# One word of padding behind each row of the output weights in SBUF

## The chip, the cores and the metric

The kernel runs on one core of one Trainium2 chip. The metric is the time of one execution on the device in microseconds; several executions are taken and their median is given. A measurement of this kernel tells apart differences of about 0.2%. One further execution was profiled; the rows below are from it.

## The reference

Three stages follow each other on 12,160 tokens (2 sequences of 6,080) of 256 features, in float32: a gated scan along each sequence, then two two-layer networks with 2,048 hidden features.

```python
sig = 1.0 / (1.0 + np.exp(-f_logit))
f = lower_bound[None, None, :] + (1.0 - lower_bound[None, None, :]) * sig
i = 1.0 - f
for t in range(S):
    h = f[:, t] * h + i[:, t] * x[:, t]
    y[:, t] = h
...
h = np.maximum(x @ w_in, 0.0)          # first network
x = h * h @ w_out
...
h = x @ w_in                           # second network
g = np.where(h > 0.0, h, np.exp(np.minimum(h, 0.0)) - 1.0)
return g @ w_out
```

## The kernel before, in words

The tokens are cut into units: the first two of 896 and 1,024 tokens (halves of 512 and 384, and of 512 and 512), the others of 1,024 tokens, taken as two halves of 512. In the second network the first unit is halved as 448 and 448. The first network of unit u and the second network of unit u - 3 alternate. Each network's hidden features are worked on in 8 groups g of 256.

TensorE does two kinds of product. Input products (`three`, line 702) multiply a tile of input weights, the ring `ws` (two buffers; in the first units a tile `s` as well), by the activations `xa` and `xb`. Output products (`add_out`, line 938) multiply the output weights `wo` by the hidden activations `g` and add into the PSUM tiles a00 to a11. All numbers are split into a high and a low part in the type float32r, so one product is three matmuls: high by high, high by low, low by high. Every matmul is one weight load of 128 x 128 (stationary operand) and one stream of 512 columns (448 or 384 in a few units) of the moving operand.

The output weights stay in SBUF for the whole kernel: two tiles, `wo0` and `wo1` (line 190), one for each network, of shape 128 x 16 x 2 x 256: for each of 16 blocks j of 128 hidden features the high part's row of 256 words and the low part's row. They are filled once, by ScalarE (high parts, line 404) and VectorE (low parts, line 410), out of the tile `a` of prepared weights. A matmul's stationary operand is half a row:

```python
wh, wl = (wo[m][:, j, x, q * P : (q + 1) * P] for x in range(2))
for p, (y, v) in enumerate(((wh, gh), (wh, gl), (wl, gh))):
    nc.tensor.matmul(a, lhsT=y, rhs=v, ...)
```

A load of 128 words is 512 bytes in each partition. Where tiles lie in SBUF follows from the order of their creation: some small constants, the tile `gap` of `GAP` words (line 187), which nothing reads or writes, then the ring `ws`, then `wo0` and `wo1`, then all other tiles. With `GAP` = 56 the ring begins at byte 2,048 of each partition, `wo0` at 16,384 and `wo1` at 49,152; a row is 1,024 bytes long. All tiles that a matmul of line 702 or 938 reads begin at a multiple of 512 bytes.

The order of the work is written by a planner (`Order`), which lists every step with an engine, a cost in us and a due time, and then gives out the steps engine by engine. Tile addresses do not enter it. For a group g its output products are 12 matmuls in a row (for each of two halves and two 128-column parts: three matmuls; in the first units for each of two parts, two blocks), and the input products stand in groups of 9 and 12.

Of the kernel before, what the change touches and what calls it, by code (L numbers as in the profile page):

```python
# [9 lines left out]
F32R = mybir.dt.float32r  # L10
# [6 lines left out]
P = 128  # L17
# [1 line left out]
CN = 256  # L19
SIZES = ((512, 384), (512, 512))  # L20
LEAD = 2
GAP = 56
BEHIND = 3
AGE = 8.0
ROW = 1 / 2258
# [127 lines left out]
def kernel(  # L153
# [12 lines left out]
    B, S, D = x.shape  # L166
# [3 lines left out]
    KF = DFF // P  # L170
# [15 lines left out]
    one = const.tile([P, P], F32, name="one")  # L186
    const.tile([P, GAP], F32, name="gap")
    pools = {"ws": ctx.enter_context(tc.tile_pool(name="ws_pool", bufs=BUFS["ws"]))}
    outer = ctx.enter_context(tc.tile_pool(name="outer", bufs=1))
    wo = [outer.tile([P, KF, 2, D], F32R, name=f"wo{m}") for m in range(2)]  # L190
    pools |= {
        tag: ctx.enter_context(tc.tile_pool(name=f"{tag}_pool", bufs=n))
        for tag, n in BUFS.items()
# [24 lines left out]
    def new(tag, shape, dtype=F32):  # L218
        return pools[tag].tile(shape, dtype, tag=tag, name=tag)
# [41 lines left out]
    for s in slots:  # L261
        m, u, h, g = s
# [20 lines left out]
    def act(n, psum=False):  # L283
        return (0.05 if psum else 0.09) + n / 1172

    def dve(n, fast=False, psum=False):
        return (0.12 if psum else 0.067) + n / (1920 if fast else 960)

    def chain(due, steps):

        left = sum(st[1] + order.SLACK for st in steps)
        for e, us, what, *rest in steps:
            order.add(e, us, due - left, what, *rest)
            left -= us + order.SLACK
# [3 lines left out]
    def key_of(tag):  # L298
        count[tag] = count.get(tag, -1) + 1
        return tag, count[tag]  # L300
# [5 lines left out]
    def load_w(queue, st, m, kind, c):  # L306
        w = ((w_in1, w_out1), (w_in2, w_out2))[m][kind].bitcast(I32)
        if kind == 1:
            v = w[c * CF : (c + 1) * CF, :].rearrange("(k p) u -> p k u", p=P)
            queue.dma_start(st.rearrange("p k e w -> p k (e w)"), v)  # L310
        elif m == 1:
            v = w[:, 2 * c * CF : 2 * (c + 1) * CF].rearrange("(k p) u -> p k u", p=P)
            queue.dma_start(st.rearrange("p k e w -> p k (e w)"), v)
        else:
            v = w[:, 2 * c * CF : 2 * (c + 1) * CF].rearrange("(p k) u -> p k u", k=KD)
            queue.dma_start(st.rearrange("p k e w -> p k (e w)"), v)

    def weight_sums(q, a):
        nc.vector.tensor_tensor(q[:, 0], a[:, 0], a[:, 2], op=ALU.add)
        nc.vector.tensor_tensor(q[:, 2], a[:, 1], a[:, 0], op=ALU.subtract)  # L320
        nc.vector.tensor_tensor(q[:, 1], q[:, 0], a[:, 1], op=ALU.subtract)
        nc.vector.tensor_tensor(q[:, 3], a[:, 3], q[:, 1], op=ALU.subtract)

    def plain_weights(key):

        if key[0] == "ws":
            return new("ws", [P, 2, NW, P], F32R)[:, :, :4]
        return new("s", [P, 3 * HN], F32R)[:, : 8 * P].rearrange("p (x k i) -> p x k i", x=2, k=4)

    def add_kept_parts(t, x, key, m, c, at, due):  # L330

        w = key_of("wp")

        def high_part(e):
            t["w" + x] = new("wp", [P, 4, P], F32R)
            if e == "ACT":
                nc.scalar.activation(t["w" + x], t[x], AF.Copy)
            else:
                nc.vector.tensor_copy(t["w" + x], t[x])

        def low_part(e):
            nc.vector.tensor_tensor(t[x].bitcast(F32R), t[x], t["w" + x].bitcast(F32), op=ALU.subtract)

        def keep(e):
            nc.sync.dma_start(wd[m][c][:, 0, at : at + 4].bitcast(F32), t["w" + x].bitcast(F32))
            nc.sync.dma_start(wd[m][c][:, 1, at : at + 4].bitcast(F32), t[x])

        chain(due, [
            ["DVE", dve(CE, True), high_part, [key], [w], ("ACT", act(CE))],
            ["DVE", dve(CE), low_part, [w], [key]],  # L350
            ["SP", 1.0, keep, [w, key], [("wd", m, c, at)], None, 512],
        ])

    def add_weights(i, m, kind, c, due, wk=None):
        t = {}

        def load(e):
            t["st"] = new("st", [P, 2, CE // 2, 2], I32)
            if i == 0:
                nc.scalar.activation(warm, warm, AF.Exp)  # L360
            load_w(nc.scalar if i == 0 else nc.sync, t["st"], m, kind, c)
            sv = t["st"].rearrange("p k e w -> p (k e) w")
            t["low"], t["high"] = sv[:, :, 0], sv[:, :, 1]

        def scaled(e):
            t["a"] = new("a", [P, 4, P])
            t["v"] = t["a"].rearrange("p q i -> p (q i)")
            t["vi"] = t["v"].bitcast(I32)
            nc.scalar.activation(t["v"], t["high"].bitcast(F32), AF.Abs, scale=2.0**-112)  # L369

        def low_bits(e):
            nc.scalar.activation(t["low"], t["low"].bitcast(U32), AF.Copy, scale=LOW_SCALE)  # L372

        def magnitude(e):
            nc.vector.scalar_tensor_tensor(t["vi"], t["vi"], 3, t["low"], op0=ALU.logical_shift_left, op1=ALU.bitwise_or)

        def sign(e):
            nc.vector.scalar_tensor_tensor(t["vi"], t["high"], -0x80000000, t["vi"], op0=ALU.bitwise_and, op1=ALU.bitwise_or)

        def sums(e):  # L380
            t["q"] = new("a", [P, 4, P])
            weight_sums(t["q"], t["a"])

        def parts():

            if kind == 0:
                return [(t["a"], ws_t[wk][:, 0], ws_t[wk][:, 1])]
            v = t["a"].rearrange("p (k e) i -> p k (e i)", k=2)
            hi, lo = (wo[m][:, 2 * c : 2 * c + 2, x, :] for x in range(2))
            if m == 0:  # L390
                return [(v, hi, lo)]

            return [
                (v[:, k].rearrange("p (a q j) -> p q a j", a=4, q=KD),
                 *(u[:, k].rearrange("p (q a j) -> p q a j", a=4, q=KD) for u in (hi, lo)))
                for k in range(2)
            ]

        def high_part(e):
            if kind == 0:  # L400
                ws_t[wk] = plain_weights(wk)
            for v, hi, _ in parts():
                if e == "ACT":
                    nc.scalar.activation(hi, v, AF.Copy)
                else:
                    nc.vector.tensor_copy(hi, v)

        def low_part(e):
            for v, hi, lo in parts():
                nc.vector.tensor_tensor(lo, v, hi.bitcast(F32), op=ALU.subtract)  # L410

        def keep(e):
            nc.sync.dma_start(wd[m][c][:, :, 0:4].bitcast(F32), ws_t[wk].bitcast(F32))

        def keep_whole(e):
            nc.sync.dma_start(rd[c], t["a"])

        st, a = ("st", i), key_of("a")
        steps = [
            ["ACT" if i == 0 else "SP", 1.0 if i == 0 else 0.475, load, (), [st], None, 512],  # L420
            ["ACT", act(CE), scaled, [st], [a]],
            ["ACT", act(CE), low_bits, (), [st]],
            ["DVE", dve(CE), magnitude, [st], [a]],
            ["DVE", dve(CE), sign, [st], [a]],
        ]
        if i == 0:
            order.add(*steps[0][:2], -20.0, *steps[0][2:])
            del steps[0]
        if m == 1 and kind == 0:
            q = key_of("a")  # L430
            chain(due - 6.0, [*steps, ["DVE", 4 * dve(P), sums, [a], [q]]])
            add_kept_parts(t, "a", a, m, c, 0, due - 2.0)
            add_kept_parts(t, "q", q, m, c, 4, due)
            return
        w = wk if kind == 0 else ("w", m, c)
        chain(due, [
            *steps,
            ["ACT", act(CE), high_part, [a], [w]],
            ["DVE", dve(CE), low_part, [a], [w]],
        ])  # L440
        if kind == 0:
            order.add("SP", 0.5, due + 16.0, keep, [w], [("wd", m, c, 0)], None, 512)
            order.add("SP", 0.5, due + 10.0, keep_whole, [a], [("rd", c)], None, 256)
# [632 lines left out]
    for kind, s in pe_order:  # L1076
# [3 lines left out]
        m, u, h, g = s  # L1080
# [38 lines left out]
```

## Time and profile before

| | |
|---|---|
| median of 3 executions | 1982.59 us (1982.42 to 1983.38) |
| the profiled execution | 1981.58 us |
| its span, first to last instruction | 1979.8 us |
| TensorE busy | 1962.0 us, 8,716 matmuls and as many weight loads |
| VectorE busy | 1673.0 us |
| ScalarE busy | 1631.8 us |
| HBM traffic | 134 GB/s over the span |

PE is TensorE's matmuls, PEld its weight loads, DVE is VectorE, ACT ScalarE, POOL GpSimd and SP SyncE. L938 is line 938 of the kernel. Matmuls overlap, and their ends are modelled in the profile: their starts are what can be measured. In the timeline a run of like instructions is one row with its start, the time to the end of its last instruction, and its count; the difference of two rows' starts is the time that the first group took on the engine. In the chain of waits a row's second number is the time of the chain that the piece took.

### The profile page before, as it was taken

The numbers are of one execution on the slowest core, as the hardware profiler recorded it, in microseconds if no ns is written. First come the engines' busy times: TensorE is split into PE (matmuls) and PEld (weight loads), VectorE is DVE, ScalarE is ACT, GpSimd is POOL, SyncE is SP. The second block draws the span as 40 slices with busy tenths as digits, with TensorE's granted clock in tenths as the row PEclk, the third lists the DMA queues.
The fourth block names the chain that finished last, engine by engine and source line by source line (L and its number), as shares of the span: only waits on it lengthen the run. The fifth ranks groups of instructions, "written<-read, shape, count | busy, mean of one in ns | idle before, by whom it ended". The sixth has DMA issues, their size and how long they took to land.

```text
span 1979.8 us, 24508 instructions
## 1 busy us (share of the span) xinstructions
PE 1962.0 (99%) x8716; PEld 1633.2 (82%) x8716; DVE 1673.0 (85%) x2292; ACT 1631.8 (82%) x2157; POOL 0.7 (0%) x6
## 2 busy tenths in 40 slices
PE   7999999999999999999999999999999999999998
PEld 6988888888888888888888888888888888888887
DVE  7889999888987987888888798798888887779886
ACT  7888998888878888888888888888887888888886
POOL 0000000000000000000000000000000000000000
PEclk9999999999999999999999999999999999999999
DMA  8877753442433443343244244334424323334231
GB/s 248 246 224 269 231 175 109 144 136 94 140 115 113 136 126 125 106 136 127 93 147 144 96 135 124 108 126 124 136 93 133 124 90 115 114 115 136 85 106 58
DMA packets 228874, 267.30 MB, mean 135 GB/s; under 512 B 151952, under 2 KB 154512, under 8 KB 228752
## 3 DMA queue, kind: packets, MB, share of 16 engines
q1 hardware_dynamic: 228480, 265.21, 42.0%
q8 instruction: 69, 1.13, 0.2%
q10 hardware_dynamic: 272, 0.52, 0.1%
q14 instruction: 53, 0.43, 0.1%
HBM read 221.91 MB, written 43.78 MB: 134 GB/s over the span
## 4 chain that ended last, share of the span: by engine, by line
PE 98%; ACT 1%; DVE 1%; DMA 0%; issue 0%; DVEq 0%; ACTq 0%
PE a L938 52%; PE c L702 46%; DMA st<-in_moe_w_in_dram 0%; ACT g L742 0%; ACT r L794 0%; DVE F L654 0%; DVE g L747 0%; ACT r L727 0%; ACT xb L481 0%; ACT st L372 0%; DVE fT L633 0%; DVE o L978 0%; DVE xT L618 0%; ACT a L369 0%; DVE r L737 0%
## 5 line engine op out<-in xcount | busy, mean ns | idle before, releaser
L938 PE MATMUL a<-g,wo 128*128 128x512 f32 (+1 forms) x4608 | 1097.3, 387 | 0.3 <-DVE g L747 0.3
L938 PEld LDWEIGHTS a<-g,wo 128*128 128x128 f32 x4608 | 863.7, 188 | 172.6 <-DVE g L747 0.7
L747 DVE TENSOR_TENSOR g<-r,g 128x1024 fp32r<-128x1024 f32 (+2 forms) x384 | 464.3, 1209 | 129.9 <-ACT g L742 129.5
L702 PE MATMUL c<-xb,ws 128*128 128x512 f32 (+2 forms) x2208 | 525.9, 387 | 0.0
L742 ACT ACTIVATE g<-r 128x1024 fp32r<-128x1024 f32 (+2 forms) x384 | 403.1, 1050 | 111.3 <-PE a L938 98.6
L702 PEld LDWEIGHTS c<-xb,ws 128*128 128x128 f32 x2208 | 413.9, 188 | 82.3 <-DVE xb L484 0.3
L702 PE MATMUL c<-xa,ws 128*128 128x512 f32 (+1 forms) x1680 | 411.7, 390 | 3.7 <-ACT xa L481 3.2
L702 PEld LDWEIGHTS c<-xa,ws 128*128 128x128 f32 x1680 | 315.4, 188 | 70.0 <-ACT xa L481 3.6
L839 ACT ACTIVATE s<-c 128x512 f32<-128x512 f32 (+1 forms) x528 | 306.9, 587 | 14.2 <-PE c L702 13.5
L737 DVE SCALAR_TENSOR_TENSOR r<-e,r 128x1024 f32<-128x1024 f32 (+1 forms) x192 | 232.4, 1210 | 32.3 <-ACT e L734 32.3
L731 ACT ACTIVATE e<-r 128x1024 f32<-128x1024 f32 (+1 forms) x192 | 201.9, 1051 | 41.1 <-DVE r L883 40.2
L727 ACT ACTIVATE r<-r 128x1024 f32<-128x1024 f32 x192 | 201.7, 1050 | 2.6
L734 ACT ACTIVATE e<-e 128x1024 f32<-128x1024 f32 (+1 forms) x192 | 201.4, 1049 | 1.8
L843 DVE TENSOR_TENSOR s<-s 128x512 f32<-128x512 f32 (+1 forms) x176 | 120.3, 684 | 73.0 <-ACT s L839 71.8
L879 ACT ACTIVATE r<-c 128x512 f32<-128x512 f32 (+1 forms) x176 | 103.9, 590 | 59.9 <-PE c L702 59.4
L876 DVE TENSOR_TENSOR s<-c,s 128x512 f32<-128x512 f32 (+1 forms) x176 | 120.7, 686 | 24.1 <-PE c L702 22.7
L887 DVE TENSOR_TENSOR r<-c,s 128x512 f32<-128x512 f32 (+1 forms) x176 | 119.8, 681 | 3.5 <-PE a L938 0.5
L883 DVE TENSOR_TENSOR r<-c,s 128x512 f32<-128x512 f32 (+1 forms) x176 | 120.3, 683 | 2.2
L890 DVE TENSOR_TENSOR r<-s 128x512 f32<-128x512 f32 (+1 forms) x176 | 119.9, 681 | 0.0
L721 ACT ACTIVATE r<-r 128x1024 f32<-128x1024 f32 x80 | 84.4, 1055 | 0.0
L724 ACT ACTIVATE r<-r 128x512 f32<-128x512 f32 x80 | 50.5, 631 | 28.3 <-DVE r L883 27.9
L654 DVE TENSOR_TENSOR_SCAN F<-fT,carry,xT 128x256 f32<-128x256 f32 (+2 forms) x94 | 66.6, 726 | 0.9
(61 smaller groups left out, 765.2 us busy)
## 6 DMA issues: line engine op xcount, KB each, us to landing
ws<-wd SPq DMA_DIRECT2D x176, 896.0 KB, 5.0
xd<-o SPq DMA_DIRECT2D x46, 256.0 KB, 5.0
fs<-in_f_logit_dram SPq DMA_DIRECT2D x176, 64.0 KB, 2.3
xs<-in_x_dram SPq DMA_DIRECT2D x176, 64.0 KB, 2.9
F<-xd SPq DMA_DIRECT2D x22, 512.0 KB, 4.6
out_dram<-o SPq DMA_DIRECT2D x88, 128.0 KB, 2.3
st<-in_moe_w_out_dram SPq DMA_DIRECT2D x16, 512.0 KB, 4.5
st<-in_moe_w_in_dram SPq DMA_DIRECT2D x15, 512.0 KB, 5.0
```

The lines of the kernel that those rows point to most:

```text
L702: nc.tensor.matmul(out, lhsT=ws[:, p, w], rhs=xs[:, r, v], start=start and q == 0, stop=stop and q == 2, skip_group_check=check,)
L727: nc.scalar.activation(r_t[0], r_t[0], AF.Square)
L731: nc.scalar.activation(t["e"], r_t[0], AF.Relu, scale=-1.0)
L734: nc.scalar.activation(t["e"], t["e"], AF.Exp, scale=-1.0)
L737: nc.vector.scalar_tensor_tensor(r_t[0], t["e"], 1.0, r_t[0], op0=ALU.subtract, op1=ALU.max)
L742: nc.scalar.activation(g_t[s, which][:, 0], r_t[0], AF.Copy)
L747: nc.vector.tensor_tensor(g_t[s, which][:, 1], r_t[0], g_t[s, which][:, 0].bitcast(F32), op=ALU.subtract)
L839: nc.scalar.activation(t["s"][:, c - 1], t[c], AF.Copy)
L843: nc.vector.tensor_tensor(t["s"][:, 1], t["s"][:, 1], t["s"][:, 2], op=ALU.add)
L876: nc.vector.tensor_tensor(t["s"][:, 0], t[0], t["s"][:, 0], op=ALU.add)
L883: nc.vector.tensor_tensor(odd[0][:, 1], t[2], t["s"][:, 0], op=ALU.add)
L938: nc.tensor.matmul(a, lhsT=y, rhs=v, start=begin and jj == 0 and p == 0, stop=end and jj == len(mine) - 1 and p == 2, skip_group_check=True,)
```

## The change

Each row of the output weights gets one word behind it that nothing reads or writes, so a row begins 257 words (1,028 bytes) after the one before. The unused tile in front of the ring `ws` grows from 56 to 120 words, by 256 bytes. The two padded tiles together are 256 bytes longer, so all tiles behind them lie 512 bytes higher than before. The ring `ws` begins at byte 2,304, `wo0` at 16,640 and `wo1` at 49,536. The written data, the instructions and their order are those of before; addresses alone differ.

```diff
@@ -19,7 +19,8 @@
 CN = 256
 SIZES = ((512, 384), (512, 512))
 LEAD = 2
-GAP = 56
+GAP = 120
+PAD = 1
 BEHIND = 3
 AGE = 8.0
 ROW = 1 / 2258
@@ -187,7 +188,7 @@
     const.tile([P, GAP], F32, name="gap")
     pools = {"ws": ctx.enter_context(tc.tile_pool(name="ws_pool", bufs=BUFS["ws"]))}
     outer = ctx.enter_context(tc.tile_pool(name="outer", bufs=1))
-    wo = [outer.tile([P, KF, 2, D], F32R, name=f"wo{m}") for m in range(2)]
+    wo = [outer.tile([P, KF, 2, D + PAD], F32R, name=f"wo{m}") for m in range(2)]
     pools |= {
         tag: ctx.enter_context(tc.tile_pool(name=f"{tag}_pool", bufs=n))
         for tag, n in BUFS.items()
@@ -386,7 +387,7 @@
             if kind == 0:
                 return [(t["a"], ws_t[wk][:, 0], ws_t[wk][:, 1])]
             v = t["a"].rearrange("p (k e) i -> p k (e i)", k=2)
-            hi, lo = (wo[m][:, 2 * c : 2 * c + 2, x, :] for x in range(2))
+            hi, lo = (wo[m][:, 2 * c : 2 * c + 2, x, :D] for x in range(2))
             if m == 0:
                 return [(v, hi, lo)]
 
```

## Rows read from the trace of the kernel before

**Rows 1.** The page: busy time of each engine, share of the span, instructions.

```profile
PE 1962.0 (99%) x8716; PEld 1633.2 (82%) x8716; DVE 1673.0 (85%) x2292; ACT 1631.8 (82%) x2157; POOL 0.7 (0%) x6
```

**Rows 2.** The page: the chain that ended last, by engine and by line.

```profile
PE 98%; ACT 1%; DVE 1%; DMA 0%; issue 0%; DVEq 0%; ACTq 0%
PE a L938 52%; PE c L702 46%; DMA st<-in_moe_w_in_dram 0%; ACT g L742 0%; ACT r L794 0%; DVE F L654 0%; DVE g L747 0%; ACT r L727 0%; ACT xb L481 0%; ACT st L372 0%; DVE fT L633 0%; DVE o L978 0%; DVE xT L618 0%; ACT a L369 0%; DVE r L737 0%
```

**Rows 3.** The page, groups: tiles, shape, count | busy us, mean ns | idle before.

```profile
L938 PE MATMUL a<-g,wo 128*128 128x512 f32 (+1 forms) x4608 | 1097.3, 387 | 0.3 <-DVE g L747 0.3
L938 PEld LDWEIGHTS a<-g,wo 128*128 128x128 f32 x4608 | 863.7, 188 | 172.6 <-DVE g L747 0.7
L702 PE MATMUL c<-xb,ws 128*128 128x512 f32 (+2 forms) x2208 | 525.9, 387 | 0.0
L702 PE MATMUL c<-xa,ws 128*128 128x512 f32 (+1 forms) x1680 | 411.7, 390 | 3.7 <-ACT xa L481 3.2
```

**Rows 4.** Timeline of TensorE, 1000 to 1030 us: start, us, instructions.

```profile
999.78 2.88 PE L938 MATMUL a<-g,wo 128*128 128x512 f32 x12
1002.50 2.20 PE L702 MATMUL c<-xa,ws 128*128 128x512 f32 x9
1004.54 2.88 PE L938 MATMUL a<-g,wo 128*128 128x512 f32 x12
1007.26 2.88 PE L702 MATMUL c<-xb,ws 128*128 128x512 f32 x12
1009.99 2.88 PE L938 MATMUL a<-g,wo 128*128 128x512 f32 x12
```

**Rows 5.** The same of 38 to 61 us: groups of 384 columns.

```profile
48.35 2.24 PE L938 MATMUL a<-g,wo 128*128 128x384 f32 x12
50.43 2.92 PE L702 MATMUL c<-xa,s 128*128 128x512 f32 x12
```

**Rows 6.** The page: granted TensorE clock in 40 slices, in tenths.

```profile
PEclk9999999999999999999999999999999999999999
```

**Rows 7.** Timeline of TensorE, 260 to 280 us: groups of 448 columns.

```profile
259.99 2.59 PE L702 MATMUL c<-xb,ws 128*128 128x448 f32 x12
262.43 2.90 PE L938 MATMUL a<-g,wo 128*128 128x512 f32 x12
...
276.72 2.59 PE L938 MATMUL a<-g,wo 128*128 128x448 f32 x12
279.15 1.18 PE L702 MATMUL c<-xb,ws 128*128 128x448 f32 x5
```

**Rows 8.** The chain in order of time, longest pieces: start, us, what.

```profile
33.38 2.72 PE a L938 x12
38.21 2.76 PE a L938 x12
...
257.41 2.75 PE a L938 x12
262.59 2.73 PE a L938 x12
267.15 2.75 PE a L938 x12
272.33 2.73 PE a L938 x12
```

**Rows 9.** All instructions on the tiles wo: ns min/median/max, first and last start.

```profile
L938 PEld LDWEIGHTS a<-g,wo x4608: 186/188/189, 33.0 to 1972.8; 128*128 128x128 f32 x192
...
L404 ACT ACTIVATE wo<-a x24: 398/418/656, 30.6 to 290.5; 128x256 fp32r<-128x256 f32 x16, 128x512 fp32r<-128x512 f32 x8
L410 DVE TENSOR_TENSOR wo<-a,wo x24: 398/422/693, 31.8 to 294.4; 128x256 fp32r<-128x256 f32 x16, 128x512 fp32r<-128x512 f32 x8
...
  ACT wo L404: 2.0, 3
...
  ACT g L742: 98.6, 171
  ACT o L964: 25.1, 12
  DVE wo L410: 2.0, 3
  DVE o L978: 0.8, 1
  DVE r L887: 0.5, 1
```

## The prediction

> **What bounds the kernel now.** I read four views in this order: the page's engine shares, the chain that ended last, the groups by line, and then the timeline of TensorE alone, where the time between two starts can be measured.
>
> TensorE is busy 99% of the span, VectorE 85%, ScalarE 82% [rows 1]. The chain says the same more strongly: 98% of it is TensorE, 52% on line 938 (output products, whose stationary operand is the tile that the change pads) and 46% on line 702 [rows 2]. Nothing waits long in front of line 938: 0.3 us in all [rows 3]. So the kernel's time is the number of matmuls times the spacing of their starts, and the question is only what the change does to that spacing. The durations in the group rows (387 ns a matmul, 188 ns a weight load) are not that spacing: matmuls overlap.
>
> The spacing comes from the timeline. In mid-kernel a group of 12 matmuls of 512 columns starts at 999.78 us after the span's start and the next group at 1002.50: 2.72 / 12 = 226.7 ns [rows 4]. Line 702 has the same: 9 matmuls from 1002.50 to 1004.54. A group of 12 with 384 columns takes 48.35 to 50.43, 173.3 ns each [rows 5]. The difference, 53.3 ns for 128 columns, is 2.4 columns per ns, the upper of the clock's two levels, and the granted clock is full throughout [rows 6]. 512 / 2.4 is 213.3 and 384 / 2.4 is 160.0, so each matmul loses 13.3 ns beside its columns, at both sizes. Every matmul has its own weight load, so I read the 13.3 ns as something between the load and the running matmul, not as a cost of columns.
>
> This loss isn't constant. Groups with 448 columns should take 186.7 + 13.3 = 200.0 ns, but take 2.44 / 12 = 203.3 on line 702 and (279.15 - 276.72) / 12 = 202.5 on line 938: about 3 ns more [rows 7]. And right behind a group with fewer columns even 512-column matmuls are slower: 2.76, 2.75 or 2.73 us for 12 in place of 2.72 (230.0, 229.2 and 227.5 ns, the last hardly more than a row's rounding) [rows 8]. So the load and the running matmul have a rhythm that costs least (13.3 ns), and out of that rhythm the same work costs 0.8 to 3.3 ns more. What sets the rhythm? The 448-column stretch is the only one whose moving rows are not a multiple of 512 bytes long (1792 = 3.5 x 512), and it is the only one that stays out of it. I take that as a hint that addresses matter. It is no more than a hint, because every tile that TensorE reads there begins at a multiple of 512 bytes.
>
> **The change part by part.**
>
> *Order and count of instructions.* Nothing moves: the same 15,802 instructions stand in the same order, and only operand addresses differ. No transfer touches the padded tiles (they are written by ScalarE and VectorE). Cost 0, and no queue is passed.
>
> *Writes into the padded tiles.* 24 ScalarE instructions of 418 ns and 24 of VectorE of 422 ns (medians), 10 us on each engine, all between 30 and 294 us [rows 9]. TensorE is not among those who waited for them; the 2.0 us are VectorE waiting for ScalarE. Even at double length they are 10 us more on engines with 15% and more to spare in the span, so I cost them at nothing; were that cover gone, the most is those 10 us.
>
> *The other tiles.* GAP grows by 64 words, so the ring of input weights ("ws") moves by 256 bytes, and everything behind the output weights by 512. The moving operands keep their place modulo 512 bytes; ws goes from 0 to 256 modulo 512. No row here shows a ws tile at another place. Bounds: nothing, or the out-of-rhythm 3.3 ns on its 3,888 matmuls, 12.8 us. I take 0, since a shift that is the same for all of them can leave a steady rhythm as it is, and keep 12.8 us for the range.
>
> *Loads of the output weights.* 4,608 of them [rows 9]. Row r of a tile (r = 2j for high parts, 2j + 1 for low parts, j from 0 to 15) begins 1028 r bytes behind a base that is a multiple of 64, so at 4r modulo 64. Only r = 0 and r = 16 stay aligned; both are high parts, each used for 192 matmuls, so 4,608 - 2 x 192 = 4,224 loads begin off a multiple of 64. The trace has no contiguous load at such an address. I bound the price from both sides by the loss that each load has now:
> - Below: the loads come into no conflict at all any more, -13.3 ns x 4,608 = -61 us.
> - Nothing: the load takes longer but is covered. A group of 384 columns keeps its 173.3 ns with the same loads, so a load has at least 226.7 - 173.3 = 53 ns to spare at 512 columns.
> - One piece more for each load: 512 bytes are 8 pieces of 64, and 9 when they begin off a multiple (that there are such pieces is an assumption). An eighth of 13.3 ns is 1.7 ns, x 4,224 = +7.0 us.
> - Rhythm lost: 0.8 to 3.3 ns x 4,608 = +3.7 to +15.2 us.
> - Above: every piece is touched twice, 13.3 ns x 4,224 = +56 us.
>
> I take the fourth, at the 2.5 ns of the 2.75 us row [rows 8], which is a group of 12 on line 938 itself and lies between the other two: 2.5 x 4,608 = +11.5 us. The reason is that the place of a row now changes every 3 to 12 matmuls, while the trace shows that a change of pattern needs a group or so to settle. The profiled execution took 1981.6 us for a span of 1979.8; the sum against it is 1993.1. The median of the runs is 1.0 us above that execution, so I forecast 1994.
>
> The Trainium skill's page "SBUF — State Buffer" (Specifications) gives lines of 16 bytes, each crossing with a penalty. By that, an unaligned load would touch 33 lines in place of 32, an estimate of a thirty-second of the loss, and the sum would be no change; no run here shows a line's size.
>
> **The rivals.**
> 1. *No change.* The load is covered: 53 ns to spare, and 188 ns shown for a load against a spacing of 226.7. For it: in thousands of mid-kernel matmuls neither the line nor the buffers matter to the spacing [rows 4]. Against it: the spacing does move by 0.8 to 3.3 ns in rows 7 and 8, so something of the load isn't covered. Time: 1982.6, give or take 4 (the 0.2% that a measurement of this kernel can tell from no change). The skill's page "TensorE: Matmul & The Clock Gate" (Step-by-step: what each phase is for) speaks for this rival: it gives the moving operand and the weight load separate read ports, so that a load takes nothing from the running matmul. The 13.3 ns beside the columns in rows 4 and 5 do not look like that.
> 2. *Faster.* Now load and moving operand begin at the same place modulo 512 bytes in every matmul, and the load starts as the matmul before it starts. If the 13.3 ns are the two meeting in the same part of the memory, rows that begin elsewhere would meet less. It decides as soon as 0.9 ns per output matmul (4 us) are won. At half the loss: 6.7 x 4,608 = 31 us, 1951.7. Against it: where the rhythm breaks in this trace it only costs.
> 3. *Far slower.* Every piece is read twice, +56 us on the median, 2039. Against it: 53 ns to spare, and the loss would have to double, not grow by a part.
> 4. *The input weights suffer too*, from their 256 bytes: 11.5 + 12.8, 2007. This is the forecast's own upper end.
> 5. *The padding does not do what it says.* The row's pitch is fixed by the tile's shape, 257 words, and the base by the tiles in front, so I give this nothing of its own.
>
> **How the numbers follow.** Rhythm or pieces lost (with rival 4): 0.41. Rival 1: 0.35. Rival 2: 0.15. Rival 3: 0.09. Slower by over 0.2% is 0.41 + 0.09 = 0.50, within it 0.35, faster 0.15. The range runs from 1975 to 2015: it takes in no change, the small half of rival 2, the pieces (1989.6), the forecast and rival 4, and leaves out rival 3 and the greater part of rival 2, some 0.2 in all. The forecast's own range is 1986.3 (0.8 ns) to 2007.
>
> **What would show it.** In the timeline of TensorE mid-kernel, the groups of 12 on line 939 (938 before) should take 2.73 to 2.76 us in place of 2.72, and those on line 703 keep 2.72 or give a little; the share of line 939 in the chain should rise from 52%. With 2.72 on both, rival 1 holds; under 2.71 on line 939, rival 2; 2.86 and more, rival 3; 2.75 on line 703, rival 4. The writes of the padded tiles may be longer without anyone on TensorE waiting for them. The forecast is wrong if the groups of 12 are unchanged, or if time has gone to a wait that this trace does not have.

## The result and the profile after

The changed kernel takes 2011.3 us (2010.89 to 2011.61, 4 runs) against 1982.51 us for the one before, a ratio of 1.0147 with a 95% interval of 1.0135 to 1.0159: 28.8 us slower. The prediction had 1994: the sign was right, but the loss is two and a half times the 11.5 us of the forecast. The time lies in the range of 1975 to 2015, and above 2007, the upper end of the forecast's own range: only the margin beyond that end takes it in.

The page of the profiled execution (span 2009.8 us, granted clock full throughout) answers to [rows 1], [rows 2] and [rows 3]. Lines after the added constant are one higher: L939 was L938, L703 was L702.

```profile
PE 1992.0 (99%) x8716; PEld 1635.2 (81%) x8716; DVE 1675.1 (83%) x2292; ACT 1632.2 (81%) x2157; POOL 0.7 (0%) x6
...
L939 PE MATMUL a<-g,wo 128*128 128x512 f32 (+1 forms) x4608 | 1119.9, 392 | 0.2 <-DVE g L748 0.2
L939 PEld LDWEIGHTS a<-g,wo 128*128 128x128 f32 x4608 | 864.5, 188 | 192.3 <-DVE g L748 0.6
...
L703 PE MATMUL c<-xb,ws 128*128 128x512 f32 (+2 forms) x2208 | 529.0, 388 | 0.0
...
L703 PE MATMUL c<-xa,ws 128*128 128x512 f32 (+1 forms) x1680 | 415.6, 392 | 3.8 <-ACT xa L482 3.4
```

TensorE is busy 30.0 us longer, which is all of the 30.0 us by which the span grew. 22.6 us of it (1119.9 - 1097.3) are on the output products, 7.0 us (3.1 + 3.9) on the input products, whose weights were not padded. Starts, which are measured, say the same: from start to start the output products take 22.5 us more and the input products 7.3. Nobody waits longer in front of a matmul: 0.2 us on L939. The weight loads themselves read the same, 188 ns.

The instructions on the padded tiles show that the fills did not matter [rows 9]:

```profile
L405 ACT ACTIVATE wo<-a x24: 397/428/662, 31.4 to 294.4; 128x256 fp32r<-128x256 f32 x16, 128x512 fp32r<-128x512 f32 x8
L411 DVE TENSOR_TENSOR wo<-a,wo x24: 400/419/693, 32.7 to 298.2; 128x256 fp32r<-128x256 f32 x16, 128x512 fp32r<-128x512 f32 x8
```

The chain in order of time, mid-kernel (start, us on the chain, what), shows where the time went:

```profile
993.88 2.79 PE a L939 x12
996.66 2.08 PE c L703 x9
998.74 2.77 PE a L939 x12
1001.51 2.75 PE c L703 x12
1004.26 2.78 PE a L939 x12
1007.04 2.05 PE c L703 x9
1009.09 2.78 PE a L939 x12
1011.87 2.72 PE c L703 x12
1014.59 2.72 PE a L939 x12
1017.31 2.04 PE c L703 x9
1019.36 2.77 PE a L939 x12
1022.12 2.72 PE c L703 x12
1024.85 2.79 PE a L939 x12
```

Before, every such group took 2.72 us (9 matmuls 2.04) [rows 4]. Now nearly every output group takes 2.77 to 2.79 (up to 2.83 elsewhere in the trace). An input group behind one sometimes takes 2.72 and sometimes 2.75. And one output group, at 1014.59, is as fast as ever. Each output group uses the high and the low row of one block j, and between 330 and 1800 us of the trace the groups of one network on the same block take the same time in every unit, within 0.003 us. So the differences belong to the rows, and to where they lie.

### The profile page after: what moved, and what is told of

It is laid out like the page before. It is cut to its first block, busy times and chain, and to the rows that moved or that the text cites. A ratio compares the mean times of both kernels' runs of the same rounds, so it can differ in the third digit from the quotient of the medians.

```text
span 2009.8 us, 24508 instructions
## 1 busy us (share of the span) xinstructions
PE 1992.0 (99%) x8716; PEld 1635.2 (81%) x8716; DVE 1675.1 (83%) x2292; ACT 1632.2 (81%) x2157; POOL 0.7 (0%) x6
## 3 DMA queue, kind: packets, MB, share of 16 engines
q8 instruction: 69, 1.13, 0.2%
## 4 chain that ended last, share of the span: by engine, by line
PE 98%; ACT 1%; DVE 1%; DMA 0%; issue 0%; DVEq 0%; ACTq 0%
PE a L939 52%; PE c L703 45%; DMA st<-in_moe_w_in_dram 0%; ACT g L743 0%; ACT r L795 0%; DVE F L655 0%; DVE g L748 0%; ACT r L728 0%; ACT st L373 0%; DVE fT L634 0%; ACT xb L482 0%; DVE o L979 0%; DVE xT L619 0%; ACT a L370 0%; DVE r L738 0%
## 5 line engine op out<-in xcount | busy, mean ns | idle before, releaser
L939 PE MATMUL a<-g,wo 128*128 128x512 f32 (+1 forms) x4608 | 1119.9, 392 | 0.2 <-DVE g L748 0.2
L939 PEld LDWEIGHTS a<-g,wo 128*128 128x128 f32 x4608 | 864.5, 188 | 192.3 <-DVE g L748 0.6
L703 PE MATMUL c<-xb,ws 128*128 128x512 f32 (+2 forms) x2208 | 529.0, 388 | 0.0
L743 ACT ACTIVATE g<-r 128x1024 fp32r<-128x1024 f32 (+2 forms) x384 | 403.2, 1050 | 139.0 <-PE a L939 129.4
L703 PEld LDWEIGHTS c<-xb,ws 128*128 128x128 f32 x2208 | 413.9, 188 | 86.5 <-DVE xb L485 0.3
L703 PE MATMUL c<-xa,ws 128*128 128x512 f32 (+1 forms) x1680 | 415.6, 392 | 3.8 <-ACT xa L482 3.4
L703 PEld LDWEIGHTS c<-xa,ws 128*128 128x128 f32 x1680 | 316.7, 189 | 73.8 <-ACT xa L482 3.8
L732 ACT ACTIVATE e<-r 128x1024 f32<-128x1024 f32 (+1 forms) x192 | 201.8, 1051 | 37.1 <-DVE r L884 36.2
```

The costliest lines, as they stand in the source:

```text
L703: nc.tensor.matmul(out, lhsT=ws[:, p, w], rhs=xs[:, r, v], start=start and q == 0, stop=stop and q == 2, skip_group_check=check,)
L732: nc.scalar.activation(t["e"], r_t[0], AF.Relu, scale=-1.0)
L743: nc.scalar.activation(g_t[s, which][:, 0], r_t[0], AF.Copy)
L939: nc.tensor.matmul(a, lhsT=y, rhs=v, start=begin and jj == 0 and p == 0, stop=end and jj == len(mine) - 1 and p == 2, skip_group_check=True,)
```

## The experiments

A *place* below is the byte at which an operand begins in its partition, counted modulo 512 and, from run 5 on, modulo 256. A place is *free*, or keeps the rhythm, if 12 matmuls with loads from it take 2.72 us, as before. Each ratio is against executions of the kernel before that were taken beside that run (medians 1981.84 to 1982.17 us).

Three theories stood at the start. **S**: what costs is that the place of the load changes from one load to the next. **O**: a load that begins off a multiple of 64 bytes costs by itself. **R**: the ring's new place has a share in it. In all kernels the moving operands stay at a multiple of 512 bytes, where needed by a spare tile behind the changed ones, unless the text says otherwise.

**1. The padding alone** (against the changed kernel).

```diff
-GAP = 120
-PAD = 1
+GAP = 56
...
-    wo = [outer.tile([P, KF, 2, D + PAD], F32R, name=f"wo{m}") for m in range(2)]
+    wo = [outer.tile([P, KF, 2, D + 1], F32R, name=f"wo{m}") for m in range(2)]
+    outer.tile([P, 64], F32, name="gap2")
```

> The padding without the ring's move: ws stays at a multiple of 512 bytes, every row of the output weights keeps its padding word. Theory S (what costs is that the place of the load changes from one load to the next, by the 4 bytes between a high row and a low row; the rhythm never settles) and theory O (each load that begins off a multiple of 64 bytes costs some 5 ns by itself) both expect the changed kernel's time, 2011 give or take 3. Theory R (the ring at 256 modulo 512 costs what groups on the input weights lose, some 1.8 ns x 3888 = 7 us) expects 2004.

Measured: 2011.18 us, ratio 1.0145 (1.0130 to 1.0161), the changed kernel's time.

**2. The ring's move alone** (this edit and all that follow are against the kernel before).

```diff
-GAP = 56
+GAP = 120
...
+    outer.tile([P, 64], F32, name="gap2")
     wo = [outer.tile([P, KF, 2, D], F32R, name=f"wo{m}") for m in range(2)]
```

> The ring's move without padding: ws at 256 modulo 512, output weights and all else at 0. S and O expect the time of before, 1982.5 give or take 2. R expects 7 us more, 1989, and up to 1995 if the two kinds of group disturb each other at every change from one to the other.

Measured: 1982.19 us, ratio 0.9999 (0.9989 to 1.0008). R has fallen. The 7 us on the input products come from the padding too: run 1, with the ring at its old place, has 529.0 and 415.9 us on its two rows of them, 7.3 more than before. Their groups start out of rhythm behind an output group and need some matmuls to settle, which is the 2.75 in the chain above; run 3 shows it inside one group.

**3. A word behind each pair of rows**, so that a block's high and low row stand at one place modulo 64.

```diff
-    wo = [outer.tile([P, KF, 2, D], F32R, name=f"wo{m}") for m in range(2)]
+    wo_t = [outer.tile([P, KF, 2 * D + 1], F32R, name=f"wo{m}") for m in range(2)]
+    wo = [w[:, :, : 2 * D].rearrange("p k (x d) -> p k x d", x=2) for w in wo_t]
+    outer.tile([P, 96], F32, name="gap2")
```

> One word of padding behind each pair of rows (high and low part of one block), so the loads of one block all stand at the same place modulo 64, 4j, and only the next block has another. S expects that a group settles within a few matmuls: 12 matmuls of the output weights in 2.72 to 2.75 us, 1983 to 1994 in all. O expects the time of the changed kernel, 15 of 16 blocks being off a multiple of 64: 2010 to 2013, 2.78 us a group.

Measured: 2006.11 us, ratio 1.0121 (1.0104 to 1.0138), between the two. The chain says more than the time:

```profile
840.27 2.78 PE a L940 x12
843.04 2.75 PE c L704 x12
845.79 2.72 PE a L940 x12
848.51 2.05 PE c L704 x9
850.56 2.78 PE a L940 x12
853.34 2.74 PE c L704 x12
856.08 2.72 PE a L940 x12
858.80 2.04 PE c L704 x9
860.84 2.72 PE a L940 x12
863.56 2.72 PE c L704 x12
866.28 2.77 PE a L940 x12
```

By the order of the blocks (the odd one of two first), the loads of these output groups begin at 124, 120, 4, 0, 12 and 8 modulo 512. Places 120, 0 and 12 keep the rhythm, and 124, 4 and 8 do not. The block at 64, a multiple of 64, takes 2.80 (the groups at that place in the trace). So neither S (one place within a group, yet no rhythm) nor O (12 and 120 are no multiples of 64, yet free) tells which.

The input group at 843.04 in this chain shows the settling. In the timeline its first matmul starts at 842.88; a second window, opened inside the group, has the rest:

```profile
842.88 2.91 PE L704 MATMUL c<-xb,ws 128*128 128x512 f32 x12
...
844.04 1.75 PE L704 MATMUL c<-xb,ws 128*128 128x512 f32 x7
845.63 0.39 PE L940 MATMUL a<-g,wo 128*128 128x512 f32 x1
```

Five matmuls take 1.16 us, 232 ns each, and the other seven 1.59, 227 ns each.

**4. All output weights 4 bytes off, no padding between rows.**

```diff
-    wo = [outer.tile([P, KF, 2, D], F32R, name=f"wo{m}") for m in range(2)]
+    wo_t = [outer.tile([P, KF * 2 * D + 16], F32R, name=f"wo{m}") for m in range(2)]
+    wo = [w[:, 1 : 1 + KF * 2 * D].rearrange("p (k x d) -> p k x d", k=KF, x=2) for w in wo_t]
+    outer.tile([P, 96], F32, name="gap2")
```

> No padding between rows; all output weights begin one word (4 bytes) behind a multiple of 64, in every row alike. S expects 1982 to 1987: nothing changes from load to load. O expects 2011 to 2014, all 4608 loads being off.

Measured: 2017.12 us, ratio 1.0175 (1.0160 to 1.0190). The first tile is 64 bytes longer than before, so the first network's loads stand at 4 and the second's at 68; their groups take 2.78 and 2.80 us in the trace. S has fallen as the cause: within a network's output products nothing changes from load to load, and it is the slowest of the four. Whether a change of place adds something of its own is taken up below. O alone is left of the three, and run 3 speaks against it.

Two new theories. **P**: what counts is where the load begins against the moving operand. **A**: the load's own place alone, whatever the moving operand's.

**5. 64 bytes behind each group of four rows**, all loads at multiples of 64.

```diff
-    wo = [outer.tile([P, KF, 2, D], F32R, name=f"wo{m}") for m in range(2)]
+    wo_t = [outer.tile([P, KG, 4 * D + 16], F32R, name=f"wo{m}") for m in range(2)]
+    wo = [[w[:, g, : 4 * D].rearrange("p (k x d) -> p k x d", k=2, x=2) for g in range(KG)] for w in wo_t]
...
```

The lines that fill and read the tiles are indexed to match.

> No padding behind rows, but 16 words (64 bytes) behind each group of 4 rows: every load begins at a multiple of 64, the groups at 0, 64, ..., 448 modulo 512. Theory O (a load off a multiple of 64 bytes costs) expects 1982.5 give or take 2. Theory P (what counts is where the load begins against the moving operand modulo 512; 0 and 256 keep the rhythm, most other places do not) expects that 6 of 8 groups of 12 matmuls take 2.77 to 2.81 us in place of 2.72: 4608 x 6/8 x 5 to 7 ns and some 5 us behind them on the input products, 2003 to 2012. Theory A (the place of the load alone, whatever the moving operand's) expects the same as P.

Measured: 2003.01 us, ratio 1.0108 (1.0093 to 1.0123). O has fallen. The chain of this run, two output groups for each place:

```profile
850.71 2.72 PE a L939 x12
...
860.91 2.80 PE a L939 x12
...
871.33 2.80 PE a L939 x12
...
881.75 2.75 PE a L939 x12
```

These are places 0, 64, 128 and 192. The four before them, 256 to 448, read 2.72, 2.80, 2.80 and 2.75 again: the cost repeats every 256 bytes. Run 1 says the same for all places in steps of 4: its output weights stand 256 bytes off, modulo 512, from those of the changed kernel, and in the two traces the groups on each block take the same time within 0.001 us.

**6. The same with 16 bytes** (4 words in place of 16, and a spare tile of 64 words).

> 4 words (16 bytes) behind each group of 4 rows: the loads of wo0 begin at 0 to 112 and those of wo1 at 128 to 240 modulo 512, all multiples of 16. O: 12 of 16 groups are off a multiple of 64: 2004 to 2008, and the groups at 0, 64, 128 and 192 keep 2.72 us. If pieces of 16 bytes count: 1982.5. P and A: all but the few places that kept the rhythm with a word behind each pair (0 and 16 among these) lose, 2006 to 2014, the groups at 64, 128 and 192 too.

Measured: 2005.95 us, ratio 1.0122 (1.0105 to 1.0139). Of the 16 places, 0, 16, 144 and 240 take 2.72 us; 64 and 128 do not. As P and A expected, and against pieces of 16 bytes.

**7 and 8. Everything at 64; the moving operands alone at 64.** The first is GAP = 72 in the kernel before and nothing else, the second a spare tile of 16 words behind the output weights.

> All tiles, weights and moving operands alike, 64 bytes higher, no padding: every load and every moving operand at 64 modulo 512. P (the place of the one against the other) expects 1982.5 give or take 2. A (the load's place alone) expects a loss of 5 to 7 ns on all 8496 matmuls, 2025 to 2040. O: 1982.5.

> All weights at 0 modulo 512, the moving operands of both kinds of product 64 bytes higher, at 64. P expects a loss on every matmul outside the first units, 5 to 7 ns x 8496: 2025 to 2040. A and O expect 1982.5 give or take 2, since no load has moved and every operand begins at a multiple of 64.

Measured: 1982.51 us, ratio 1.0004 (0.9995 to 1.0013), and 1998.87 us, ratio 1.0085 (1.0070 to 1.0100). A has fallen, since a load at 64 costs nothing when the moving operand is there too, and moving that operand alone costs although no load of `wo` or `ws` has moved. P's sign was right and its size wrong: I had reckoned with the cost of place 64, but a load at 0 stands at -64, that is 192, against a moving operand at 64. That place cost 2.75 us for 12 in run 5, and the timeline of run 8 has it for both products, 1001.89 to 1004.63 to 1007.38:

```profile
1001.89 2.91 PE L939 MATMUL a<-g,wo 128*128 128x512 f32 x12
1004.63 2.91 PE L703 MATMUL c<-xb,ws 128*128 128x512 f32 x12
1007.38 2.91 PE L939 MATMUL a<-g,wo 128*128 128x512 f32 x12
```

**9. All output weights 16 bytes off** (run 4 with 4 words in place of 1 and 64 words more in each tile, so that both tiles are at 16 modulo 256).

> All output weights begin 16 bytes behind a multiple of 256, in every row alike; moving operands and ring as before. Theory P, now with a period of 256 bytes (places 64 and 320, 128 and 384, 192 and 448 cost the same), expects that place 16 keeps the rhythm: 2.72 us a group, 1982.5 give or take 2. Theory O (a load off a multiple of 64 costs) expects 2011 to 2017.

Measured: 1983.56 us, ratio 1.0008 (0.9998 to 1.0017). As P expected.

**10. Output weights and hidden activations both 4 bytes off** (run 9's edit with 1 word in place of 4, and this one).

```diff
-            g_t[s, which] = new("g", [P, 2, 2, HN], F32R)[:, :, :, :n]
+            whole = new("g", [P, 4 * HN + 64], F32R)[:, 1 : 1 + 4 * HN]
+            g_t[s, which] = whole.rearrange("p (x k i) -> p x k i", x=2, k=2)[:, :, :, :n]
```

> Output weights and the hidden activations that are multiplied with them both begin 4 bytes behind a multiple of 256; the input products as before. P expects 1982.5 give or take 3, although all 4608 loads stand where they stood in the run with 4 bytes' offset alone, which took 2017: the place of the one against the other is 0. O and A expect 2015 to 2017, and more where ScalarE and VectorE are slower on the shifted tile.

Measured: 2040.86 us, ratio 1.0298 (1.0283 to 1.0313): a miss for all. The two stand at 0 against each other, and an output group takes 2.84 us, more than any place had cost:

```profile
1001.11 3.00 PE L940 MATMUL a<-g,wo 128*128 128x512 f32 x12
1003.95 2.93 PE L703 MATMUL c<-xb,ws 128*128 128x512 f32 x12
```

Only half of the loads, those of the first network, stand where they stood in run 4; the second network's were at 68 there. No wait explains it: in front of the output products TensorE idles for 0.0 us in all, and ScalarE and VectorE write the shifted tile at 1,051 and 1,209 ns an instruction, against 1,050 and 1,209 before. Something was still missing from P.

**11. The moving operands at 192** (run 8 with 48 words).

> All weights at 0, the moving operands of both products at 192: the load's place against them is 64 modulo 256, which took 233.2 ns a matmul where groups were 64 bytes apart, against 228.9 at 192. P expects 233.2 - 226.7 = 6.5 ns x 8496 = 55 us: 2034 to 2040, 2.80 us for each group of 12 of either product. Were it the distance of 64 bytes alone that counts, with the moving operand before or behind: 1999 as at 64.

Measured: 2034.81 us, ratio 1.0267 (1.0252 to 1.0283), and 2.80 us for 12 on both products, as P expected of place 64 seen from the other side:

```profile
1001.19 2.96 PE L703 MATMUL c<-xb,ws 128*128 128x512 f32 x12
1003.99 2.96 PE L939 MATMUL a<-g,wo 128*128 128x512 f32 x12
1006.79 2.26 PE L703 MATMUL c<-xa,ws 128*128 128x512 f32 x9
```

**12. The other half of the places** (run 3 behind a spare tile of 32 words, and 64 words after).

> A word behind each pair of rows as in the third run, but the places now run in steps of 4 bytes from 128 to 188 and from 192 to 252, so that with that run all 64 places modulo 256 are seen. P expects 2000 to 2008 by the places known so far, and that 144 and 240 keep 2.72 us. The question beside it: does any place take less than 2.72 us for 12? Nothing so far says so; if one does, a kernel with all loads at that place beats the kernel before.

Measured: 2007.95 us, ratio 1.0131 (1.0116 to 1.0146). With run 3 all 64 places modulo 256 have been seen. 16 of them take 2.72 us for 12 (0, 12, 16, 28, 36, 40, 100, 120, 132, 144, 156, 216, 228, 240, 244, 252), none takes less, the slowest (164) takes 2.84, and the mean over the 64 is 2.774 us. So no place beats the kernel before. The chain of this run at the places 240, 252 and 164:

```profile
1003.29 2.72 PE a L941 x12
1008.05 2.72 PE a L941 x12
...
1059.60 2.84 PE a L941 x12
```

**13 to 15. The moving operand's own place**, left open by run 10. 13 is run 10's edit of the hidden activations alone; 14 is GAP = 64 in the kernel before, everything at 32; 15 is run 10 with 4 words (16 bytes) in both.

> Only the hidden activations are 4 bytes off, all weights at 0. Theory P (the place of the load against the moving operand alone) expects that 252 modulo 256, which kept the rhythm or nearly, keeps it: 1982 to 1986. Theory M (a moving operand that begins off a multiple of 64 costs some 10 ns by itself) expects what both 4 off gave: 2030 to 2042.

> All tiles 32 bytes higher: loads and moving operands at 32, place 0 against each other. P expects 1982.5 give or take 2. M with 64 bytes expects 10 ns x 8496 = 85 us more, 2067; M with pieces of 32 or 16 bytes expects 1982.5.

> Output weights and hidden activations both 16 bytes off. P expects 1982.5 give or take 2. M with 64 or 32 bytes expects 2030 to 2042; M with 16 bytes expects 1982.5.

Measured: 2030.74 us, ratio 1.0245 (1.0228 to 1.0262); 1983.51 us, ratio 1.0009 (1.0000 to 1.0019); 2004.93 us, ratio 1.0115 (1.0100 to 1.0130). The timelines of 13 and of 15, of which the first group's start and the next row's give the time:

```profile
1002.76 3.01 PE L939 MATMUL a<-g,wo 128*128 128x512 f32 x12
1005.61 2.21 PE L702 MATMUL c<-xa,ws 128*128 128x512 f32 x9
```

```profile
1000.34 2.92 PE L940 MATMUL a<-g,wo 128*128 128x512 f32 x12
1003.10 2.23 PE L703 MATMUL c<-xa,ws 128*128 128x512 f32 x9
```

With the moving operand 4 bytes off, the 12 take 2.85 us (237 ns each), with both 16 off 2.76 (230 ns), with everything 32 off 2.72. In 13 the loads stand at 252 against the moving operand, in 10, 14 and 15 at 0, and both places are free in the map of run 12. So a moving operand that is 4 or 16 bytes off a multiple of 32 has a cost of its own: M, with a size that depends on how far it is off; 15 lies below what a fixed 10 ns would give. Other loads' places against such an operand were not tried, so P is shown for moving operands at 0, 32, 64 and 192 alone. The changed kernel has no such operand, so this second effect has no share in its 28.8 us.

## Why the prediction was right or wrong

*The frame held.* TensorE's spacing sets the time, the order did not change, the fills and all waits cost nothing, the padded rows' loads disturb a rhythm between load and moving operand. All 30 us of the span are in matmul spacing.

*The step that failed is the size of the rhythm term*, "2.5 ns x 4,608 = +11.5 us", with its upper end of 3.3 ns. It measured 22.6 us / 4,608 = 4.9 ns, and the groups of 12 that were to take 2.73 to 2.76 us take mostly 2.77 to 2.79. I took the price from groups of 512 columns behind shorter ones [rows 8], which all stood at place 0: they lost the rhythm once and found it again within the 12 matmuls, so their mean was diluted by the settled part. The row of 2.75 us itself, from which the 2.5 ns came, shows it in the timeline before, again with a second window opened inside the group:

```profile
257.24 2.91 PE L938 MATMUL a<-g,wo 128*128 128x512 f32 x12
...
258.86 1.30 PE L938 MATMUL a<-g,wo 128*128 128x512 f32 x5
259.99 0.36 PE L702 MATMUL c<-xb,ws 128*128 128x448 f32 x1
```

Its first seven matmuls took 1.62 us, 231 ns each, and the other five 1.13, the 226.7 ns of the rhythm within rounding. Out of the rhythm a matmul cost nearly 5 ns more even there.

The reason given for the price failed too. The place of a row does not change "every 3 to 12 matmuls": the three matmuls of a product load high, high, low, so it changes after every one or two, and no group has the time to settle that rows 8 show. Nor is a change needed. At most of the new places there is no rhythm to find: each place has its own steady cost, as in run 11, where mid-kernel all loads have one place and all moving operands another, and every group of 12 takes 2.80 us. The mean of all 64 places, 2.774 us, alone gives (2.774 - 2.720) / 12 = 4.5 ns.

High and low row stand 4 bytes apart, so a group of the changed kernel goes through two places. Of the 32 pairs (8k, 8k + 4) just one is free in both, by the list of run 12: 240 and 244. It is the group at 1014.59 in the chain after, whose rows begin at 496 and 500 modulo 512, and no other block's group keeps 2.72. Beyond that the map does not give a pair's cost. The traces have both: rows at 128 and 132 take 2.82 us together, where groups at one of these places alone took 2.80 and 2.72, and rows at 160 and 164 take 2.77, where those took 2.80 and 2.84. Of the 32 pairs 7 lie above both of their places and 9 below both. Only the average is near: 2.784 us measured, 2.773 by two loads at the high row's place for each at the low row's. So a group that alternates between two places is not a mixture of two steady ones, and what sets its cost is open.

*The second failed step is the zero for the input weights.* They lose 7.0 us, 1.8 ns on 3,888 matmuls. The prediction had this as rival 4, at 2007, but for the wrong reason: not the ring's place (run 2), but the output group in front, behind which each input group has to find its rhythm again. So 2.75 us on line 703, which was to be the sign of rival 4, did appear without its cause.

*The hint from the 448 columns misled in its number.* "Modulo 512" should be 256 (run 5), and 448 columns are 1,792 bytes, which is a multiple of 256. Why those groups stay out of the rhythm is open; it was not tried.

*The other rivals.* No change: the 53 ns to spare did not cover it, because the cost is not the load's length (188 ns, as before) but where the load stands against the moving operand. The page "TensorE: Matmul & The Clock Gate" of the Trainium skill (Step-by-step: what each phase is for) gives the two separate read ports, so that a load takes nothing from the running matmul; runs 7, 8 and 11 have the same instructions at other places and take 1982.5, 1998.9 and 2034.8 us by where the two operands stand against each other, so here the measurement decides against it. Faster: the idea that place against place counts was right, but place 0 is already one of the 16 cheapest, and none is cheaper. Far slower: no place costs 13.3 ns more; the worst of the 64 costs 9.8 (2.838 us). Pieces of 64 bytes fell with run 5, and lines of 16 with run 6, where all loads begin on one and 12 of the 16 places are slow.

## What to carry to other kernels

When TensorE sets the time and every matmul loads new weights, compare the spacing of matmul starts with the columns, and look at the addresses of both operands. In this kernel nothing beat weights and moving operand at the same place modulo 256 bytes with the moving operand at a multiple of 32; other shapes and types were not tried. Padding a weight row by a word, which spreads the rows over all places, slowed the groups of 31 of the 32 blocks (16 in each network). And a mean over a disturbance that heals is too low a price for one that does not: read the disturbed part alone.

## What was not expected of the hardware

With float32r operands and a new load for every matmul, the cost of a weight load depends on its place against the moving operand with a period of 256 bytes: from 226.7 ns a matmul of 512 columns at 16 of the 64 places to 236.5 ns at the worst, the same whether the load or the moving operand is shifted (229 ns at 192 in runs 5 and 8, 233 ns at 64 in runs 5 and 11). With the moving operand alone 4 bytes off it is 237 ns. Through all of this the load's own mean duration reads 187 to 189 ns; only the spacing of the starts shows the loss. Which part of the chip makes the two collide, and why just these 16 places are free, no run here shows.
